# Splitting x into high and low parts at other places, and a later first y for 256 columns, in an attention and two-layer MoE kernel

## The chip, the cores and the metric

One Trainium2 chip, one core of it. The metric is the device time of one execution in microseconds (us); lower is better.

## What is computed

Attention with a window, and behind it two dense layers of the form y = g(x @ w_in) @ w_out, all in float32:

```python
# q, k, v: (4, 8, 576, 64)
scores = scale * np.matmul(q, k.transpose(0, 1, 3, 2))
mask = (rel >= 0) & (rel < 128)
scores = np.where(mask, scores + bias[None], -1000000000.0)
attn = np.exp(scores - np.max(scores, axis=-1, keepdims=True))
attn = attn / (np.sum(attn, axis=-1, keepdims=True) + 1e-09)
x = np.matmul(attn, v)            # -> x: (2304, 512)
h = x @ w_in;  x = (h * np.cos(h)) @ w_out          # first layer, 512 -> 2048 -> 512
h = x @ w_in2
g = np.where(h >= 1, h, np.where(h <= -1, 0.0, (h + 1) ** 2 / 4.0))
out = g @ w_out2
```

## The kernel before

**Attention.** The work is cut into 36 pairs: two blocks of 128 tokens and two heads. `pairs[n]` has b0 = 2 (n // 4) and hp = n % 4. The loop of `attention()` runs in steps k from -3 to 31, each of which holds four pairs in different stages, and its last pair (35) and what is left of pairs 31 to 34 are written out by hand behind the loop (the tail, p0 to p4 = pairs 31 to 35). In step k:

- PE: `pe_s` (L248) the scores of pair k + 3, `pe_t` (L288) eight transposes of the attention weights of pair k, `pe_v` (L313) the outputs of pair k - 1;
- DVE: `scores` (L263) adds the bias and takes the maximum of pair k + 3 in two halves; ACT makes the exponentials (L270) with their sums in st;
- `prepare` (L446, POOL) adds 1e-9 to the sums, `invert` (L451, DVE) takes the reciprocal, `normalise` (L276, POOL) multiplies, two instructions a pair;
- `copy_t` (L297 ACT, L299 DVE) brings the transposes out of PSUM as pt, by the string PT;
- `put_x` (L333 ACT, L335 DVE) brings the output of pair k - 1 out of PSUM into x;
- `make(0)` in the steps of D_STEPS does one piece of the first layer's weights (below).

For k < 1 the three of `prepare`, `invert` and `normalise` stand between the two halves of `scores` (L481 to L485).

**x in two parts.** A float32 matmul is done as three matmuls of a high part (float32r, rounded) and the low part (what is left): hi x hi, hi x lo, lo x hi. The first layer's first pass (`chunks[0]`) takes 768 columns: part 0 of 512 (tokens of pairs 0 to 7) and part 1 of 256 (pairs 8 to 11), each in four tiles d. For part 1, `put_x` writes the high part on ACT straight out of PSUM (L326) and `sub_lo` (L81, DVE) the low part behind it, in the same step (k = 9 to 12). For part 0, `split_x` (ACT cast L353, DVE L81) does both parts of one d. The low parts of part 0 lie where the bias tables lie that pairs with hp = d still need, so d = 0 and 1 are split in steps 30 and 31, and d = 2 and 3 in the tail.

**The first pass.** `moes()` runs f = 0 to 15 over blocks of 128 of the 2048. For each f: `mm_a` of part 0 (L375, h, 12 matmuls of 512 columns), `chain` of part 0 (ACT L387 k, DVE L389, ACT L391 sine, DVE L393 t, ACT L405 gh, DVE L81 gl), `mm_b` of part 0 for f - 1 (L425, y, 12 matmuls), then the same of part 1 with 256 columns (one tile g for both parts; `mm_b` 12 matmuls). PSUM has eight banks, y0 to y3 and h0 to h3. Part 1's y lies in h2 and h3, but for f = 1 part 0's h lies in h3 too:

```python
            tag = "h3" if f == 1 and i == 0 else f"h{i}"
```

Between these stand `slot()` and `make(0)`: pieces of the weights, which come as 64-bit numbers and are made float32 and split (DVE L125, L131, L135, L81; ACT L114, L140), eight pieces for each f. Their loads (L91) are issued on SP and need a buffer that L135 frees. All other chunks follow behind the first pass and run the same way with 512 columns.

**What sets the order.** `manual_schedule` keeps the instructions of PE, DVE, ACT, POOL and SP as they are written; each engine runs its own in that order, and waits where a tile isn't ready or its buffer not free.

Of the kernel before, what the change touches and what calls it, by code (L numbers as in the profile page):

```python
# [43 lines left out]
def attention_moe_moe_kernel(  # L44
# [35 lines left out]
    def sub_lo(eng, out, full, hi):  # L80
        eng.tensor_tensor(out=out, in0=full, in1=f32(hi), op=ALU.subtract)  # L81
# [114 lines left out]
    def new_x(w, dtype=F32):  # L196
        size = w if x_free[w] else 512
        slot = size, x_free[size].pop(0)
        return one.tile([128, size], dtype, tag=f"x{size}.{slot[1]}", name=nm("x"))[:, 0:w], slot
# [115 lines left out]
                              start=(i == 0), stop=(i == nb - 1))  # L315

    evicted = [0]

    def put_x(p, eng=None):
        t0 = p["b0"] * 128  # L320
        o, w = max(a for a in all_parts if a[0] <= t0)
        if (o, w) == chunks[0]["parts"][1]:
            hi, slot = new_x(w, F32R)
            lo = x_lo(4 + p["hp"])
            chunks[0]["xs", 1, p["hp"]] = hi, lo, slot
            ACT.copy(hi, p["vb"][:, 0:256])  # L326
            sub_lo(DVE, lo, p["vb"][:, 0:256], hi)
            return
        if (o, p["hp"]) not in x_tiles:
            x_tiles[o, p["hp"]] = new_x(w)  # L330
        x = x_tiles[o, p["hp"]][0][:, t0 - o:t0 - o + 256]
        if (eng or XE[evicted[0] % len(XE)]) == "A":
            ACT.copy(x, p["vb"][:, 0:256])  # L333
        else:
            DVE.tensor_copy(x, p["vb"][:, 0:256])  # L335
        evicted[0] += 1
# [8 lines left out]
            free_x(c["xs", i, d][2])  # L345

    def split_x(c, i, ds):
        o, w = c["parts"][i]
        for d in ds:
            x, slot = x_tiles.pop((o, d))  # L350
            hi, hi_slot = new_x(w, F32R)
            lo = x_lo(4 * i + d)[:, 0:w]
            ACT.copy(hi, x)  # L353
            sub_lo(DVE, lo, x, hi)
            free_x(slot)
            c["xs", i, d] = hi, lo, hi_slot

    h_no = [-1]

# [93 lines left out]
    def attention():  # L453
        qk, v = slice(0, 640), slice(640, 1024)
        for part in (qk, v):
            for n in range(3):
                load(n, part)
        make_identity(nc, ident)
        make_dist8()
        DVE.memset(half, 0.5)  # L460
        DVE.memset(half_pi, TWO_PI / 4)
        np_ = len(pairs)
        c0 = chunks[0]
        for k in range(-AHEAD, np_ - AHEAD - 1):
            new = pairs[k + AHEAD]
            mid = pairs[k + AHEAD - 1] if k + AHEAD >= 1 else None
            nrm = pairs[k + AHEAD - 2] if k >= 2 else None
            cur = pairs[k] if k >= 0 else None
            old = pairs[k - 1] if k >= 1 else None
            if k > -AHEAD:  # L470
                load(k + AHEAD + 1)
                load(k + AHEAD + 2)
            if k == 0:
                pe_t(cur)
            pe_s(new)
            if k > 0:
                pe_t(cur)
            if old:
                pe_v(old)
            scores(new, 0)  # L480
            if k < 1 and mid:  # L481

                prepare(mid)
                invert(mid)
                normalise(mid)  # L485
            if cur:
                copy_t(cur, 0)
            if nrm:
                normalise(nrm)
            if k >= 1:  # L490
                prepare(mid)
            scores(new, 1)

            if k in D_STEPS:
                make(0)
            if k in (np_ - 6, np_ - 5):
                split_x(c0, 0, [k - (np_ - 6)])
            if k >= 1:
                invert(mid)
            if cur:  # L500
                copy_t(cur, 1)
            if k + 1 == D_STEPS[0]:
                start(0)
            if old:
                put_x(old)

        p0, p1, p2, p3, p4 = pairs[np_ - 5:]
        pe_s(p4)
        pe_t(p1)
        pe_v(p0)  # L510
        scores(p4, 0)
        copy_t(p1, 0, "D")
        normalise(p2)
        invert(p3, add=True)
        normalise(p3)
        copy_t(p1, 1, "A")
        scores(p4, 1)
        pe_t(p2)
        pe_v(p1)
        copy_t(p2, 0, "D")  # L520

        ACT.activation(half_pi2, half, AF.Sin)
        put_x(p0, "A")
        invert(p4, add=True)
        normalise(p4)
        copy_t(p2, 1, "D")
        pe_t(p3)
        pe_v(p2)
        split_x(c0, 0, [2])
        put_x(p1, "D")  # L530
        copy_t(p3, 0, "D")
        copy_t(p3, 1, "A")
        pe_t(p4)
        pe_v(p3)
        put_x(p2, "A")
        split_x(c0, 0, [3])
        copy_t(p4, 0, "D")
        copy_t(p4, 1, "A")
        make(0)
        make(0)  # L540
        pe_v(p4)
        put_x(p3, "A")
        for _ in range(D_TAIL - 2):
            make(0)
        put_x(p4, "A")

    def moes():
# [7 lines left out]
        for f in range(NF):  # L555
# [16 lines left out]
                free_xs(c0, 1)  # L572
            while made[0] < min(N_W1, 8 * f + 9):
                make(0)
            if f:
                mm_b(c0, 1, f - 1)
        carried = c0
        step = 0
        for ci, c in enumerate(chunks[1:], 1):
# [81 lines left out]
```

## Time and profile before

| | |
|---|---|
| median of 3 runs | 930.52 us (930.34 to 932.04) |
| profiled execution | 930.21 us, its span 928.4 us |
| busy, share of the span | PE 98%, DVE 59%, ACT 47%, POOL 13% |
| attention, up to the first matmul of the first pass | 127.84 us |
| DMA queue of the loads, share of 16 engines | 22.9% |
| granted TensorE clock | 0.999 |

Times in the rows below are microseconds from the span's start. A row of a timeline gives start, duration, engine, line, operation, the tile written <- the tiles read, the shape, how many instructions were merged, and in brackets how long the engine stood before it and what ended that.

### The profile page before, as it was taken

How to read it: one execution, taken by the hardware profiler on the slowest of the kernel's cores; microseconds unless marked ns; L12 is line 12 of the kernel's file. 1: busy time of each engine (PE TensorE's matmuls, PEld its weight loads, DVE VectorE, ACT ScalarE, POOL GpSimd, SP SyncE). 2: the span in 40 equal slices, each digit the busy share in tenths (PEclk: the TensorE clock that was granted, in tenths of full speed). 3: DMA queues.
4: the chain of work that ended last, by engine and by line, in shares of the span. 5: the costliest groups of instructions: out<-in, count | busy, mean ns of one | idle time of the engine just before them, and what ended most of it. 6: DMA issues, size and time to landing. Idle time of an engine off the chain costs nothing.

```text
span 928.4 us, 13106 instructions
## 1 busy us (share of the span) xinstructions
PE 909.6 (98%) x4944; PEld 755.2 (81%) x4944; DVE 551.6 (59%) x1192; ACT 435.2 (47%) x923; POOL 120.8 (13%) x147
## 2 busy tenths in 40 slices
PE   7999988999999999999999999999999999999998
PEld 5767777888888888888888888888888888888898
DVE  6888788888868667767433543344344334433443
ACT  7788865665655444444455532232233223322332
POOL 5666620000000000000144510000000000000000
PEclk9999999999999999999999999999999999999999
DMA  9346013333305443542322200010001000100100
GB/s 355 145 168 265 2 67 116 116 128 120 116 34 191 136 151 122 170 137 92 102 100 104 69 1 1 0 46 1 1 1 45 1 1 1 46 0 1 39 9 23
DMA packets 24687, 74.77 MB, mean 81 GB/s; under 512 B 2736, under 2 KB 3632, under 8 KB 24624
## 3 DMA queue, kind: packets, MB, share of 16 engines
q1 hardware_dynamic: 24624, 73.94, 22.9%
q8 instruction: 39, 0.64, 0.3%
q14 instruction: 24, 0.20, 0.1%
HBM read 60.82 MB, written 13.11 MB: 80 GB/s over the span
## 4 chain that ended last, share of the span: by engine, by line
PE 79%; DVE 10%; ACT 8%; issue 2%; POOL 0%; DMA 0%; ACTq 0%; DVEq 0%
PE y L425 36%; PE h L375 36%; PE pa L248 2%; PE pa L288 2%; PE pa L313 2%; DVE wu L131 2%; ACT t L391 2%; ACT sc L270 2%; DVE t L393 1%; ACT wh L140 1%; DVE wl L81 1%; DVE gl L81 1%; DVE wu L135 1%; ACT wu L114 1%; ACT gh L405 1%
## 5 line engine op out<-in xcount | busy, mean ns | idle before, releaser
L375 PE MATMUL h<-x,wh 128*128 128x512 f32 (+1 forms) x640 | 237.0, 370 | 1.0
L375 PE MATMUL h<-xl,wh 128*128 128x512 f32 (+1 forms) x640 | 235.6, 368 | 0.0
L375 PE MATMUL h<-x,wl 128*128 128x512 f32 (+1 forms) x640 | 235.5, 368 | 0.0
L425 PE MATMUL y<-gl,wh 128*128 128x512 f32 (+1 forms) x576 | 217.5, 378 | 0.4 <-DVE gl L81 0.4
L425 PE MATMUL y<-gh,wh 128*128 128x512 f32 (+1 forms) x576 | 217.3, 377 | 0.0
L425 PE MATMUL y<-gh,wl 128*128 128x512 f32 (+1 forms) x576 | 217.3, 377 | 0.0
L396 ACT ACTIVATE t<-t,half 128x512 f32<-128x512 f32 (+1 forms) x80 | 54.4, 680 | 189.7 <-DVE t L395 189.4
L375 PEld LDWEIGHTS h<-x,wh 128*128 128x128 f32 x640 | 120.6, 188 | 23.6 <-DVE t L393 3.2
L375 PEld LDWEIGHTS h<-x,wl 128*128 128x128 f32 x640 | 120.7, 189 | 20.3
L375 PEld LDWEIGHTS h<-xl,wh 128*128 128x128 f32 x640 | 120.6, 188 | 20.1
L81 DVE TENSOR_TENSOR gl<-t,gh 128x512 fp32r<-128x512 f32 (+1 forms) x144 | 95.5, 663 | 68.3 <-ACT gh L405 64.1
L405 ACT CAST gh<-t 128x512 fp32r<-128x512 f32 (+1 forms) x144 | 86.0, 597 | 105.0 <-DVE t L398 56.4
L425 PEld LDWEIGHTS y<-gl,wh 128*128 128x128 f32 x576 | 108.5, 188 | 21.0 <-DVE gl L81 1.1
L425 PEld LDWEIGHTS y<-gh,wh 128*128 128x128 f32 x576 | 108.4, 188 | 20.0
L425 PEld LDWEIGHTS y<-gh,wl 128*128 128x128 f32 x576 | 108.3, 188 | 19.9
L395 DVE TENSOR_SCALAR t<-h 128x512 f32<-128x512 f32 (+1 forms) x80 | 50.9, 636 | 88.9 <-PE h L375 88.8
L81 POOL TENSOR_TENSOR wl<-wst,wh 128x512 fp32r<-128x512 f32 x32 | 41.1, 1308 | 372.6 <-ACT wh L182 372.6
L398 DVE TENSOR_TENSOR t<-h,t 128x512 f32<-128x512 f32 (+1 forms) x80 | 51.1, 638 | 61.8 <-ACT t L396 61.8
L391 ACT ACTIVATE t<-t,half_pi 128x512 f32<-128x512 f32 x80 | 54.6, 682 | 62.6 <-DVE t L389 62.6
L389 DVE SCALAR_TENSOR_TENSOR t<-h,k 128x512 f32<-128x512 f32 x80 | 50.8, 635 | 54.6 <-ACT k L387 54.4
L270 ACT ACTIVATE sc<-sc,st 128x256 f32<-128x256 f32 (+1 forms) x144 | 70.2, 489 | 23.9 <-DVE st L263 20.5
L276 POOL TENSOR_TENSOR sc<-sc,st 128x512 f32<-128x512 f32 (+1 forms) x72 | 70.0, 994 | 35.3 <-DVE st L451 30.5
(56 smaller groups left out, 853.1 us busy)
## 6 DMA issues: line engine op xcount, KB each, us to landing
wst<-in_w SPq DMA_DIRECT2D x64, 512.0 KB, 3.7
qkv<-in_qkv SPq DMA_DIRECT2D x33, 512.0 KB, 9.4
wd<-wu SPq DMA_DIRECT2D x32, 256.0 KB, 2.4
wst<-wd SPq DMA_DIRECT2D x16, 512.0 KB, 3.3
out_t<-ys SPq DMA_DIRECT2D x16, 256.0 KB, 2.1
qkv<-in_qkv SPq DMA_DIRECT2D x3, 320.0 KB, 3.6
qkv<-in_qkv SPq DMA_DIRECT2D x3, 192.0 KB, 5.1
out_t<-ys SPq DMA_DIRECT2D x4, 128.0 KB, 1.8
```

What stands on the lines that cost most here:

```text
L81: eng.tensor_tensor(out=out, in0=full, in1=f32(hi), op=ALU.subtract)
L131: DVE.scalar_tensor_tensor(out=ui, in0=high, scalar=0x80000000, in1=ui, op0=ALU.bitwise_and, op1=ALU.bitwise_or)
L270: ACT.activation(sc[:, h, 0:w], sc[:, h, 0:w], AF.Exp, bias=st[:, c:c + 1], scale=-1.0, accum_out=st[:, 4 + c:5 + c])
L276: POOL.tensor_tensor(out=sc[:, :, 0:w], in0=sc[:, :, 0:w], in1=st[:, 8 + 2 * j:10 + 2 * j].unsqueeze(2).to_broadcast([128, 2, w]), op=ALU. ...
L375: PE.matmul(h, lhsT=a[:, 0, s], rhs=x, start=(n == 0), stop=(n == 11))
L389: DVE.scalar_tensor_tensor(out=t, in0=h, scalar=INV_2PI, in1=k, op0=ALU.mult, op1=ALU.subtract)
L391: ACT.activation(t, t, AF.Sin, bias=half_pi, scale=TWO_PI)
L395: DVE.tensor_scalar(out=t, in0=h, scalar1=-1.0, scalar2=1.0, op0=ALU.max, op1=ALU.min)
L396: ACT.activation(t, t, AF.Square, bias=half, scale=0.5)
L398: DVE.tensor_tensor(out=t, in0=h, in1=t, op=ALU.max)
L405: ACT.copy(gh, t)
L425: PE.matmul(c["y", i][d], lhsT=a[:, 1, s], rhs=x, start=(f == 0 and k == 0 and not (i and d % 2)), stop=(f == NF - 1 and k == 2 and (i == ...
```

## The change

Five edits, all in the order of instructions:

- for k < 1, the sum of 1e-9 is done on DVE (`invert(mid, add=True)`) and stands with the reciprocal and POOL's product behind both halves of `scores`;
- the low parts of part 1 are put on a list and done in the next step, behind the second half of `scores` and the piece of weights;
- `split_x` is cut into `split_hi` (ACT's cast) and what it returns (`rest`, DVE's low part). The casts of d = 0, 1, 2 stand at the ends of steps 29, 30, 31; the low parts of 0 and 1 in steps 30 and 31;
- in the tail the low parts of 2 and 3 stand behind the last copies, and one piece of weights stands before these copies. There are still five pieces in the tail;
- in the first pass `mm_b` of part 1 for f - 1 = 0 isn't done in f = 1 but in f = 2, before that for f - 1 = 1.

```diff
--- before.py
+++ after.py
@@ -315,6 +315,7 @@
                               start=(i == 0), stop=(i == nb - 1))
 
     evicted = [0]
+    low_parts = []
 
     def put_x(p, eng=None):
         t0 = p["b0"] * 128
@@ -324,7 +325,7 @@
             lo = x_lo(4 + p["hp"])
             chunks[0]["xs", 1, p["hp"]] = hi, lo, slot
             ACT.copy(hi, p["vb"][:, 0:256])
-            sub_lo(DVE, lo, p["vb"][:, 0:256], hi)
+            low_parts.append(lambda: sub_lo(DVE, lo, p["vb"][:, 0:256], hi))
             return
         if (o, p["hp"]) not in x_tiles:
             x_tiles[o, p["hp"]] = new_x(w)
@@ -345,15 +346,23 @@
             free_x(c["xs", i, d][2])
 
     def split_x(c, i, ds):
+        for d in ds:
+            split_hi(c, i, d)()
+
+    def split_hi(c, i, d):
+
         o, w = c["parts"][i]
-        for d in ds:
-            x, slot = x_tiles.pop((o, d))
-            hi, hi_slot = new_x(w, F32R)
+        x, slot = x_tiles.pop((o, d))
+        hi, hi_slot = new_x(w, F32R)
+        ACT.copy(hi, x)
+
+        def rest():
             lo = x_lo(4 * i + d)[:, 0:w]
-            ACT.copy(hi, x)
             sub_lo(DVE, lo, x, hi)
             free_x(slot)
             c["xs", i, d] = hi, lo, hi_slot
+
+        return rest
 
     h_no = [-1]
 
@@ -478,11 +487,6 @@
             if old:
                 pe_v(old)
             scores(new, 0)
-            if k < 1 and mid:
-
-                prepare(mid)
-                invert(mid)
-                normalise(mid)
             if cur:
                 copy_t(cur, 0)
             if nrm:
@@ -493,17 +497,23 @@
 
             if k in D_STEPS:
                 make(0)
-            if k in (np_ - 6, np_ - 5):
-                split_x(c0, 0, [k - (np_ - 6)])
-            if k >= 1:
-                invert(mid)
+            while low_parts:
+                low_parts.pop()()
+            if mid:
+                invert(mid, add=k < 1)
+                if k < 1:
+
+                    normalise(mid)
             if cur:
                 copy_t(cur, 1)
             if k + 1 == D_STEPS[0]:
                 start(0)
             if old:
                 put_x(old)
-
+            if k >= np_ - 7:
+                low_parts.append(split_hi(c0, 0, k - (np_ - 7)))
+
+        x2, = low_parts
         p0, p1, p2, p3, p4 = pairs[np_ - 5:]
         pe_s(p4)
         pe_t(p1)
@@ -526,20 +536,21 @@
         copy_t(p2, 1, "D")
         pe_t(p3)
         pe_v(p2)
-        split_x(c0, 0, [2])
         put_x(p1, "D")
         copy_t(p3, 0, "D")
         copy_t(p3, 1, "A")
         pe_t(p4)
         pe_v(p3)
         put_x(p2, "A")
-        split_x(c0, 0, [3])
+        make(0)
         copy_t(p4, 0, "D")
         copy_t(p4, 1, "A")
+        x2()
+        pe_v(p4)
+        x3 = split_hi(c0, 0, 3)
+        put_x(p3, "A")
         make(0)
-        make(0)
-        pe_v(p4)
-        put_x(p3, "A")
+        x3()
         for _ in range(D_TAIL - 2):
             make(0)
         put_x(p4, "A")
@@ -572,8 +583,8 @@
                 free_xs(c0, 1)
             while made[0] < min(N_W1, 8 * f + 9):
                 make(0)
-            if f:
-                mm_b(c0, 1, f - 1)
+            for g in (f - 2, f - 1) if f == 2 else (f - 1,) if f > 2 else ():
+                mm_b(c0, 1, g)
         carried = c0
         step = 0
         for ci, c in enumerate(chunks[1:], 1):
```

Line numbers of the changed kernel are up to ten higher (L81 is the same; L451 is L460, L450 L459, L335 L336, L375 L384, L425 L434).

DVE in step 11, from the last scores of pair 14 on (sc and st are tiles of `scores`, xl are low parts of x, wu and wst weights). Before:

```order
L135 SCALAR_TENSOR_TENSOR wu_355<-wst_353,wu_355 128x512
L451 RECIPROCAL st_679<-st_679 128x4
L299 COPY pt_781<-pa_745 128x512
L81 TENSOR_TENSOR xl_784<-pa_750,x_783 128x256
L263 ISA sc_817,st_789<-pa_790,xl_108 128x256
```

And now:

```order
L135 SCALAR_TENSOR_TENSOR wu_355<-wst_353,wu_355 128x512
L81 TENSOR_TENSOR xl_726<-pa_697,x_725 128x256
L460 RECIPROCAL st_678<-st_678 128x4
L299 COPY pt_781<-pa_744 128x512
L263 ISA sc_816,st_788<-pa_789,xl_108 128x256
```

The low part of pair 10 (xl_784) is gone from this step's end, and that of pair 9 (xl_726), whose high part ACT made in the step before, stands in front of the reciprocal.

DVE in the tail, from the second copy of pair 33 on (pt are copies, x_1692 is x of a later chunk, xl_1898 and xl_1927 or xl_1929 and xl_1949 the low parts of d = 2 and 3). Before:

```order
L299 COPY pt_1876<-pa_1853 128x512
L81 TENSOR_TENSOR xl_1898<-x_357,x_1897 128x512
L335 COPY x_1692<-pa_1858 128x256
L299 COPY pt_1902<-pa_1878 128x512
L81 TENSOR_TENSOR xl_1927<-x_410,x_1926 128x512
L299 COPY pt_1930<-pa_1906 128x512
L131 SCALAR_TENSOR_TENSOR wu_1037<-wst_404,wu_1037 128x512
```

And now:

```order
L299 COPY pt_1878<-pa_1855 128x512
L336 COPY x_1692<-pa_1860 128x256
L299 COPY pt_1900<-pa_1880 128x512
L131 SCALAR_TENSOR_TENSOR wu_1037<-wst_404,wu_1037 128x512
L299 COPY pt_1925<-pa_1904 128x512
L81 TENSOR_TENSOR xl_1929<-x_357,x_1800 128x512
L135 SCALAR_TENSOR_TENSOR wu_1037<-wst_404,wu_1037 128x512
L81 TENSOR_TENSOR xl_1949<-x_410,x_1940 128x512
```

No low part stands between the copies that PE's transposes and outputs wait for; one piece of weights (L131) stands there.

PE in the first pass, f = 2, from the last matmul of part 1's h on (y_2183 and y_2184 hold part 1's y, g_2017 is g of f = 0 and g_2098 that of f = 1). Now:

```order
L384 MATMUL h_2149<-x_835,wl_2014 128x256
L434 MATMUL y_2183<-g_2017,wh_776 128x256 x2
L434 MATMUL y_2183<-g_2017,wl_777 128x256
L434 MATMUL y_2183<-g_2017,wh_776 128x256 x2
L434 MATMUL y_2183<-g_2017,wl_777 128x256
L434 MATMUL y_2184<-g_2017,wh_776 128x256 x2
```

Before, the twelve matmuls of g_2017 stood in f = 1, right in front of h of f = 2; now h of f = 2 and y of part 0 run first.

## Rows read from the trace of the kernel before

**Rows 1.** The page's first part, PE: busy us, share of the span, instructions.

```profile
PE 909.6 (98%) x4944; PEld 755.2 (81%) x4944; DVE 551.6 (59%) x1192; ACT 435.2 (47%) x923; POOL 120.8 (13%) x147
```

**Rows 2.** Waits in 0 to 125 us: total, times, longest.

```profile
DVE xl L81 <- ACT x L326: 4.7, 4, 1.5
DVE xl L81 <- ACT x L353: 3.5, 3, 1.4
PE pa L288 <- DVE pt L299: 3.3, 3, 1.5
DVE st L451 <- POOL st L446: 2.7, 4, 1.0
```

**Rows 3.** Timeline of PE: first scores of steps 10, 15, 28 and 29.

```profile
41.00 1.13 PE L248 MATMUL pa<-qkv 64*128 64x256 f32 x8
...
59.79 0.92 PE L248 MATMUL pa<-qkv 64*128 64x256 f32 x8
...
100.55 1.13 PE L248 MATMUL pa<-qkv 64*128 64x256 f32 x8
...
103.67 1.13 PE L248 MATMUL pa<-qkv 64*128 64x256 f32 x8
```

**Rows 4.** Timeline of DVE: steps 9, 14 and 29.

```profile
42.29 0.42 DVE L81 TENSOR_TENSOR xl<-pa,x 128x256 fp32r<-128x256 f32 x1 [0.89 <-ACT x L326]
...
59.24 0.81 DVE L81 TENSOR_TENSOR wl<-wu,wh 128x512 fp32r<-128x512 f32 x1
...
104.40 0.42 DVE L263 CUSTOM_DVE_ANT_0 sc<-pa,xl 128x256 f32<-128x256 f32 x1 [0.52 <-PE pa L248]
```

**Rows 5.** Timeline of all engines, steps 0 and 1.

```profile
11.89 0.18 DVE L451 RECIPROCAL st<-st 128x4 f32<-128x4 f32 x1 [0.88 <-POOL st L446]
...
13.76 0.56 ACT L297 COPY pt<-pa 128x512 f32<-128x512 f32 x1
...
14.46 0.63 PE L288 MATMUL pa<-ident,sc 128*128 128x128 f32 x4 [0.28 <-ACT pt L297]
```

**Rows 6.** Timeline of all engines, steps 30 and 31 and the tail.

```profile
111.35 0.69 DVE L81 TENSOR_TENSOR xl<-x,x 128x512 fp32r<-128x512 f32 x1 [1.39 <-ACT x L353]
...
118.29 0.16 DVE L450 TENSOR_SCALAR st<-st 128x4 f32<-128x4 f32 x1
...
118.83 2.04 POOL L276 TENSOR_TENSOR sc<-sc,st 128x512 f32<-128x512 f32 x2 [0.46 <-DVE st L451]
...
120.19 1.28 ACT L522 ACT_TABLE_LOAD   x1
120.20 0.70 DVE L450 TENSOR_SCALAR st<-st 128x4 f32<-128x4 f32 x1 [0.28 <-ACT sc L270]
...
122.50 1.37 DVE L81 TENSOR_TENSOR xl<-x,x 128x512 fp32r<-128x512 f32 x1 [0.81 <-ACT x L353]
...
127.84 0.50 PE L375 MATMUL h<-x,wh 128*128 128x512 f32 x1
```

**Rows 7.** Timeline of PE in the first pass, f = 1 and 2.

```profile
142.75 0.50 PE L425 MATMUL y<-g,wh 128*128 128x256 f32 x2 [2.38 <-DVE t L393]
...
143.56 0.39 PE L375 MATMUL h<-x,wh 128*128 128x512 f32 x1
...
146.31 0.39 PE L425 MATMUL y<-gh,wh 128*128 128x512 f32 x1
```

**Rows 8.** Timeline of DVE in the first pass, f = 1, 2 and 13.

```profile
143.49 0.69 DVE L81 TENSOR_TENSOR gl<-t,gh 128x512 fp32r<-128x512 f32 x1 [0.20 <-issue]
...
150.82 0.69 DVE L393 TENSOR_TENSOR t<-h,t 128x512 f32<-128x512 f32 x1 [0.46 <-ACT t L391]
...
246.62 0.69 DVE L393 TENSOR_TENSOR t<-h,t 128x512 f32<-128x512 f32 x1 [0.46 <-ACT t L391]
```

**Rows 9.** Waits in 125 to 300 us: total, times, longest.

```profile
PEld h L375 <- DVE t L393: 3.2, 11, 0.3
```

**Rows 10.** Waits of SP's queue in 0 to 300 us: total, times, longest.

```profile
SPq L91 <- DVE wu L135: 206.8, 32, 51.3
```

## The prediction

> **What bounds the kernel now.** I read the page's first part first: PE is busy 909.6 of 928.4 us [rows 1]. That says PE, but the ends of matmuls are modelled, so a busy PE can hide waiting. So I went to the waits of two stretches, and from the longest of them to the timelines.
>
> In attention (to 127.84 us) DVE stands 4.7 us until ACT has cast the high parts of the 256 columns, 3.5 us for those of the 512 columns, and 2.7 us until POOL has added 1e-9; PE stands 3.3 us for DVE's copies pt [rows 2]. A step without such a wait takes PE 3.12 us (100.55 to 103.67). Steps 10 to 14, from 41.00 to 59.79, take 18.79 us instead of 5 x 3.12 = 15.60 [rows 3]. These are the steps in which DVE stands in front of the low part, with the next scores queued behind it [rows 4].
>
> In the first pass PE has one long stall, 2.38 us, in the first y of the 256 columns [rows 7], and 11 short ones, 3.2 us in all, each at the first matmul of a new f, until DVE's t (L393) has left h's bank [rows 9]. That L393 starts at 150.82 in f = 2 and at 246.62 in f = 13: 95.80/11 = 8.71 us a step [rows 8]. PE's own work is 24 matmuls of 0.229 us (12 run from 143.56 to 146.31 [rows 7]) and 24 of half of that: 8.25 us. So from f = 0 on the pace is that of DVE and ACT, which hand t, g and the weights to each other, and PE waits for them. Whatever time the pass ends is set by when that loop starts.
>
> **The change part by part.**
>
> Start (k < 1). The sum of 1e-9 moves from POOL to DVE and, with the reciprocal, behind the second scores. DVE's 0.88 us in front of the reciprocal at 11.89 go, and the reciprocal leaves that place [rows 5]. Then PE's first transposes, which need POOL's product, come some 0.1 later, as the reciprocal now stands behind two more scores. Pair 3's second scores come 0.9 earlier, so do ACT's exponentials and the copy at 13.76 [rows 5], and with it PE's transposes at 14.46, which had stood 0.28 for it. Ends: 0.3 (PE's own stall) and 2.7 (all of DVE's wait [rows 2]). I take **0.9**, nearest to the one wait that stands in front of PE; the others are covered by ACT's queue.
>
> The 256 columns (steps 9 to 13). Four low parts of 0.42 move one step on, behind the second scores. DVE's four waits, 4.7 us, go; the 0.42 are paid as before. Followed with the rows' durations: in step 10 the scores start at 41.7, not behind the low part of 42.29 (DVE starts scores 0.73 behind PE's matmuls, 104.40 against 103.67 [rows 3, 4]); step 10's scores end at 44.1, so PE's next scores find their banks free; step 12 starts at 47.2, step 13 at 50.5, step 14 at 53.7, step 15 at 56.6 instead of 59.79. In step 13 PE still stands some 0.2 for ACT's copy. The low part now holds the bank of v's output a step longer; that bank is written again two steps later, and each low part is done more than 1 us before that. ACT's hi is not moved here. Ends: 3.2 (18.79 to 15.60), and 0.8 if the slow steps belong to their three pieces of weight work, at most 0.81 each [rows 4]: 3.2 - 2.4. I take **3.1**, by the followed steps.
>
> The 512 columns (step 29 to the end of attention). The casts of d = 0, 1, 2 go to ACT one step sooner, the low parts of 0 and 1 stand behind the second scores, those of 2 and 3 behind the last copies. In step 30 DVE is through with its scores at 111.35 - 1.39 = 109.96 [rows 6]: low part to 110.6, reciprocal to 110.7, 1.3 sooner. ACT's copy no longer stands behind the cast, so PE's next transposes come 0.4 sooner. In step 31 DVE's low part ends at 113.6 and its last copy at 114.3; PE has pair 32's second transposes at 114.7. Then DVE's copies follow each other with no low part between them. Two holds stay: the 1e-9 for the last pair waits for POOL's products to about 118.4, and pair 34's second copy for the bank behind it. ACT's table load of 1.28 stays, from 117.8, where ACT isn't awaited. PE ends the outputs of pairs 34 and 35 at 122.9 and 123.95 and starts the pass there, not at 127.84. Low part 2 ends at 122.8 and 3 at 124.0, before the pass's 8th and 11th matmul want them. The five pieces of weights are the same five, so 14 pieces are made when the pass starts, as before.
> Check from above: from 103.67 [rows 3] to 127.84 [rows 6] PE has three steps of 3.12 and a tail of one scores, four transposes and five outputs of pairs, ten thirds of 3.12: 19.8 of 24.2 us, so 4.4 is the high end. Low end: PE's 3.3 us for pt [rows 2] less the table load 1.28: 2.0. I take **3.9** as followed, near the high end because PE then hardly waits.
> All that is moved starts the loop of the first pass as much earlier: its first L389 waits for the first h.
>
> The first pass. mm_b of the 256 columns for f = 0 (12 matmuls, 1.4 us) goes behind f = 2's; no instruction is added. The 2.38 go. In the times of before PE then starts h for f = 2 at 139.5 and is through at 142.2; next is y of the 512 columns of f = 1, whose gl DVE makes at 143.49 to 144.18 [rows 8]: a new wait of 1.2 for gh and 0.5 for gl. With the moved 1.4 us paid in f = 2, PE comes to h of f = 3 at about 151.0; L393 of f = 2 ends at 151.45, and at 151.9 PE starts it now. From there L393 of f = 3 decides, and no instruction of DVE or ACT in that loop waits for PE's y. Ends: 0, and 2.38 if the loop could follow. I take **0**: the stall is cut up and handed on.
>
> The sum: 0.9 + 3.1 + 3.9 + 0 = 7.9 us. The profiled execution took 930.21; that gives 922.3. It lies 0.31 below the median of the three runs, 930.52, so I give **922.6**. SP is passed by nothing: its loads for the weights wait for DVE to free their buffers (206.8 us [rows 10]), so they come earlier with it.
>
> **A rule against the change.** The sum moved to DVE, and every low part of 512 columns, runs beside POOL's products: the same 1e-9 on DVE took 0.16 at 118.29 and 0.70 at 120.20, ending as POOL's pair from 118.83 (2.04) ended; the same low part took 0.69 at 111.35 and 1.37 at 122.50 [rows 6]. The Trainium skill, "SBUF — State Buffer", section "Who interferes with whom", says why: VectorE's second port belongs to GpSimd too, and the second to come is blocked for the whole instruction. The trace agrees. In my sum stand two such holds, of 0.5 each (start and tail), neither of which ends last. By the rule alone each would be paid in full, 6.9 in place of 7.9.
>
> **The rivals.**
> 1. *The stall of 2.38 comes off as well*, because DVE and ACT could follow a PE that doesn't stop in f = 1. For it: PE is 98% busy [rows 1], and this is its longest stall behind the first load. Against it: 8.71 us a step over eleven steps, with DVE and ACT alone in the loop [rows 8]. 930.5 - 7.9 - 2.4 = 920.2. It is what the Trainium skill's "Perfetto Trace Analysis", section "Optimization Strategy", would have one expect, which looks for the gaps of the most contended engine.
> 2. *Attention gives back half.* The weight work, not the low part, paces steps 11 to 14, ACT's table load gets into the tail's way, and the start yields only PE's own stall: the low ends 0.3 + 0.8 + 2.0 = 3.1, so 927.4. For it: three of the five slow steps do carry weight work. Against: the four DVE waits lie in exactly the slow steps.
> 3. *Slower, by POOL's hold.* One mechanism: DVE comes to a moved instruction while POOL's pair of products runs, and stands up to 2.04 us, with scores and copies queued behind. Seven can be hit (three sums, four low parts from SBUF): 14.3 us at most. It turns the sign if more than 7.9/14.3 = 55% of that is paid on the path; if 90%, 12.9: 935.5. Against: POOL starts right behind the reciprocal and ends 2.1 later, while the low part stands two scores and a copy behind, 2.3 in the followed step 31.
> 4. *No change.* The pass could run by the arrival of its weights and not by its start, 930.5. Against: SP's loads wait for DVE, not the other way [rows 10].
>
> **How the numbers follow.** Forecast 0.72, rival 1 0.08, rival 2 0.10, rival 3 0.04, rival 4 0.06. The range of the forecast is what its parts leave open, about 3 us either way: 919.5 holds rival 1, 926.0 a part of rival 2. Less than 0.2% (1.9 us) a measurement of this kernel can't tell from nothing: faster 0.72 + 0.08 + 0.10 = 0.90, same 0.06, slower 0.04.
>
> **What the new profile would show.** Right: DVE no longer waits for ACT's casts of x in attention; steps 10 to 14 take under 16 us; the first matmul of the pass stands near 120 us; the stall of 2.38 is gone, a wait for gh and gl of 1 to 2 us stands in f = 2, and L393 still comes every 8.7 us. Wrong: a first matmul later than 123.5, a step of the pass other than 8.7, or long sums and low parts on DVE beside POOL.

## The result

| | before | after |
|---|---|---|
| median | 931.25 us (930.34 to 932.04, 4 runs) | 923.47 us (923.07 to 924.23, 4 runs) |
| profiled execution | 930.21 us, span 928.4 | 923.45 us, span 921.7 |
| attention, to the first matmul of the first pass | 127.84 us | 121.05 us |

The changed kernel is faster: ratio 0.9918, 95% interval 0.9901 to 0.9935. Forecast were 922.6 us and a range of 919.5 to 926.0. An execution of the kernel before takes near 930.4 or near 932.0 us, so it is luck that the medians lie 7.78 apart, close to the 7.9 forecast; the profiled executions lie 6.76 apart. Attention holds 6.79.

The page's first part, after (beside [rows 1]):

```profile
PE 907.9 (99%) x4944; PEld 754.5 (82%) x4944; DVE 553.3 (60%) x1195; ACT 434.4 (47%) x923; POOL 120.4 (13%) x144
```

PE's busy time falls by 1.7 us and the span by 6.7, so the number that says "98% busy" hardly moved. Timeline of PE, after: first scores of steps 2 ("the third step" of the expectations, counted from k = 0), 10, 15 and 29, and the first matmul of the first pass (columns as in [rows 3]):

```profile
16.02 1.13 PE L248 MATMUL pa<-qkv 64*128 64x256 f32 x8
...
41.20 1.14 PE L248 MATMUL pa<-qkv 64*128 64x256 f32 x8
...
56.90 0.92 PE L248 MATMUL pa<-qkv 64*128 64x256 f32 x8
...
100.78 1.13 PE L248 MATMUL pa<-qkv 64*128 64x256 f32 x8
...
121.05 0.50 PE L384 MATMUL h<-x,wh 128*128 128x512 f32 x1
```

Steps 10 to 14 take 15.70 us, where they took 18.79 [rows 3]: 3.09 gained. From step 29 to the first pass it is 20.27, where it was 24.17 [rows 3, 6]: 3.90 gained. At step 10 the kernel is 0.20 later than before (41.20 for 41.00): that is the start, and it was lost, not won. Waits of DVE in 0 to 125 us, after:

```profile
DVE sc L263 <- PE pa L248: 5.1, 11, 1.7
DVE pt L299 <- PE pa L288: 3.6, 13, 0.6
```

The 4.7 and 3.5 us for ACT's casts and the 2.7 for POOL's sum [rows 2] are gone from the list; DVE waits for PE, somewhat longer than before (3.0 and 3.0 us). The first pass, after: timeline of PE in f = 2, then of DVE (t, once L393, is now L402) in f = 2 and 13.

```profile
136.67 0.50 PE L434 MATMUL y<-gh,wh 128*128 128x512 f32 x1 [1.06 <-ACT gh L414]
...
137.45 0.50 PE L434 MATMUL y<-gl,wh 128*128 128x512 f32 x1 [0.28 <-DVE gl L81]
```

```profile
144.04 0.69 DVE L402 TENSOR_TENSOR t<-h,t 128x512 f32<-128x512 f32 x1 [0.46 <-ACT t L400]
...
239.85 0.69 DVE L402 TENSOR_TENSOR t<-h,t 128x512 f32<-128x512 f32 x1 [0.46 <-ACT t L400]
```

PE's stall of 2.38 [rows 7] has become 1.06 + 0.28; the step is (239.85 - 144.04)/11 = 8.71 us, as before [rows 8]. The pass starts 6.79 earlier (121.05 for 127.84) and its f = 13 is reached 6.77 earlier.

### The profile page after: what moved, and what is told of

Its sections match the earlier page's. It is cut to its first block, busy times and chain, and to the rows that moved or that the text cites. A ratio compares the mean times of both kernels' runs of the same rounds, so it can differ in the third digit from the quotient of the medians.

```text
span 921.7 us, 13110 instructions
## 1 busy us (share of the span) xinstructions
PE 907.9 (99%) x4944; PEld 754.5 (82%) x4944; DVE 553.3 (60%) x1195; ACT 434.4 (47%) x923; POOL 120.4 (13%) x144
## 4 chain that ended last, share of the span: by engine, by line
PE 81%; DVE 8%; ACT 6%; issue 2%; DMA 1%; SPq 0%; POOL 0%; ACTq 0%; DVEq 0%; POOLq 0%
PE y L434 36%; PE h L384 36%; PE pa L248 3%; PE pa L288 3%; PE pa L313 3%; DVE wu L131 2%; ACT t L400 2%; DMA qkv<-in_qkv 1%; DVE t L402 1%; DVE wl L81 1%; DVE gl L81 1%; DVE wu L135 1%; ACT wh L140 1%; ACT gh L414 1%; ACT wu L114 1%
## 5 line engine op out<-in xcount | busy, mean ns | idle before, releaser
L384 PE MATMUL h<-x,wh 128*128 128x512 f32 (+1 forms) x640 | 237.1, 370 | 1.3 <-DVE t L402 0.2
L384 PE MATMUL h<-xl,wh 128*128 128x512 f32 (+1 forms) x640 | 235.6, 368 | 0.0
L384 PE MATMUL h<-x,wl 128*128 128x512 f32 (+1 forms) x640 | 235.5, 368 | 0.0
L434 PE MATMUL y<-gh,wh 128*128 128x512 f32 (+1 forms) x576 | 217.4, 378 | 1.1 <-ACT gh L414 1.1
L434 PE MATMUL y<-gl,wh 128*128 128x512 f32 (+1 forms) x576 | 217.6, 378 | 0.6 <-DVE gl L81 0.6
L434 PE MATMUL y<-gh,wl 128*128 128x512 f32 (+1 forms) x576 | 217.3, 377 | 0.0
L384 PEld LDWEIGHTS h<-x,wh 128*128 128x128 f32 x640 | 120.6, 189 | 24.3 <-DVE t L402 3.9
L384 PEld LDWEIGHTS h<-x,wl 128*128 128x128 f32 x640 | 120.6, 188 | 20.3
L384 PEld LDWEIGHTS h<-xl,wh 128*128 128x128 f32 x640 | 120.6, 188 | 20.0
L81 DVE TENSOR_TENSOR gl<-t,gh 128x512 fp32r<-128x512 f32 (+1 forms) x144 | 95.5, 663 | 68.3 <-ACT gh L414 64.1
L434 PEld LDWEIGHTS y<-gl,wh 128*128 128x128 f32 x576 | 108.4, 188 | 21.6 <-DVE gl L81 1.7
L434 PEld LDWEIGHTS y<-gh,wh 128*128 128x128 f32 x576 | 108.3, 188 | 21.5 <-ACT gh L414 1.5
L434 PEld LDWEIGHTS y<-gh,wl 128*128 128x128 f32 x576 | 108.4, 188 | 19.8
L81 POOL TENSOR_TENSOR wl<-wst,wh 128x512 fp32r<-128x512 f32 x32 | 41.1, 1309 | 371.1 <-ACT wh L182 371.1
L398 DVE SCALAR_TENSOR_TENSOR t<-h,k 128x512 f32<-128x512 f32 x80 | 50.8, 635 | 53.9 <-ACT k L396 53.7
```

Source lines behind the costliest of these rows:

```text
L384: PE.matmul(h, lhsT=a[:, 0, s], rhs=x, start=(n == 0), stop=(n == 11))
L398: DVE.scalar_tensor_tensor(out=t, in0=h, scalar=INV_2PI, in1=k, op0=ALU.mult, op1=ALU.subtract)
L434: PE.matmul(c["y", i][d], lhsT=a[:, 1, s], rhs=x, start=(f == 0 and k == 0 and not (i and d % 2)), stop=(f == NF - 1 and k == 2 and (i == ...
```

## The experiments

Theory: three waits of DVE were in front of PE in attention, each part of the change takes its own, and the first pass is paced by DVE and ACT, so that it only starts earlier. Open: why the start lost 0.2 where 0.9 were forecast. Eleven kernels ran. Times of one group were taken on one chip beside the kernel before (medians there 930.94, 930.33 and 930.42).

### One part undone at a time

**start_undone**

```diff
+            if k < 1 and mid:
+                prepare(mid)
+                invert(mid)
+                normalise(mid)
             if cur:
                 copy_t(cur, 0)
...
-            if mid:
-                invert(mid, add=k < 1)
-                if k < 1:
-                    normalise(mid)
+            if k >= 1:
+                invert(mid)
```

> The changed kernel with its start put back: for the first three pairs the sum of 1e-9 on POOL, the reciprocal and the products stand between the two halves of the scores again. Read from the changed kernel's chain: POOL's product of pair 0 starts 0.35 later (8.08 for 7.73), since the reciprocal now stands behind pair 1's second scores and DVE's own sum, PE's transposes of pair 0 and with them pair 3's scores come later, and the third step starts at 16.02 in place of 15.83. This theory: 0.2 us faster than the changed kernel (923.3 for 923.5), third step at 15.83 again, first matmul of the first pass at 120.85. The prediction's term (the new start is worth 0.9): slower, 924.4, third step near 16.9. Rival 2's low end (0.3): 923.8.

**cols256_undone**

```diff
-            low_parts.append(lambda: sub_lo(DVE, lo, p["vb"][:, 0:256], hi))
+            sub_lo(DVE, lo, p["vb"][:, 0:256], hi)
```

> The changed kernel with the four low parts of the 256 columns back behind their casts, in the step of the cast. The prediction (that wait alone is the 3.1 us of steps 10 to 14): those five steps take 18.8 us again in place of 15.7, first matmul of the first pass at 124.1 in place of 121.05, time 926.6. Rival 2 (weight work paces these steps): at most 0.8 slower, 924.3. If the parts of the change share one wait, less than 3.1 here and the rest elsewhere.

**cols512_undone**

```diff
             while low_parts:
                 low_parts.pop()()
+            if k in (np_ - 6, np_ - 5):
+                split_x(c0, 0, [k - (np_ - 6)])
...
-            if k >= np_ - 7:
-                low_parts.append(split_hi(c0, 0, k - (np_ - 7)))
...
+        split_x(c0, 0, [2])
         put_x(p1, "D")
...
+        split_x(c0, 0, [3])
         copy_t(p4, 0, "D")
         copy_t(p4, 1, "A")
-        x2()
+        make(0)
+        make(0)
         pe_v(p4)
-        x3 = split_hi(c0, 0, 3)
         put_x(p3, "A")
-        make(0)
-        x3()
```

> The changed kernel with the casts and low parts of the 512 columns where they stood before (casts of d = 0 and 1 a step later with the low part behind them, d = 2 and 3 between the last copies). The prediction: 3.9 us slower, 927.4, steps up to 29 unchanged, first matmul of the first pass at 124.95. Rival 2 (the table load and the last copies pace the tail): 2.0 slower, 925.5.

**defer_undone**

```diff
-            for g in (f - 2, f - 1) if f == 2 else (f - 1,) if f > 2 else ():
-                mm_b(c0, 1, g)
+            if f:
+                mm_b(c0, 1, f - 1)
```

> The changed kernel with y of the 256 columns for f = 0 back in f = 1. The prediction (the loop of DVE and ACT paces the pass): no difference, 923.5 within 0.3; PE's stall of some 2.4 us in f = 1 is back, the waits for gh and gl in f = 2 (1.06 and 0.28) are gone, t (L402) still every 8.71 us and at 239.85 in f = 13. Rival 1 (the stall comes off the time): 2.4 slower, 925.9.

Measured, with the start of step 2 and of the first pass's first matmul in each profile:

| kernel | median us | ratio to before | 95% | step 2 | first matmul | between |
|---|---|---|---|---|---|---|
| before | 931.25 | | | 15.83 | 127.84 | 112.01 |
| after | 923.47 | 0.9918 | 0.9901 to 0.9935 | 16.02 | 121.05 | 105.03 |
| start_undone | 923.75 | 0.9925 | 0.9913 to 0.9938 | 16.02 | 121.06 | 105.04 |
| cols256_undone | 925.90 | 0.9950 | 0.9937 to 0.9962 | 15.04 | 123.18 | 108.14 |
| cols512_undone | 927.12 | 0.9960 | 0.9947 to 0.9972 | 16.90 | 125.83 | 108.93 |
| defer_undone | 922.88 | 0.9910 | 0.9895 to 0.9925 | 16.28 | 121.32 | 105.04 |

The last column settles the two large terms. Without the new place of the 256 columns' low parts it is 3.11 us longer, without that of the 512 columns 3.90; 3.11 + 3.90 = 7.01, and before it was 6.98 longer: the terms add, neither shares a wait with the other. Rival 2's low ends (0.8 and 2.0) fall. The times alone would not show this so well: the profiled executions of the two (925.68 and 928.20) are 2.23 and 4.75 slower than that of the changed kernel, since their starts are 0.98 sooner and 0.88 later. Timelines of PE, of cols256_undone (steps 10 and 15) and then of cols512_undone (step 31, the tail's scores 3.58 behind it where a free step takes 3.12, and the first matmul):

```profile
40.24 1.13 PE L248 MATMUL pa<-qkv 64*128 64x256 f32 x8
...
59.03 0.92 PE L248 MATMUL pa<-qkv 64*128 64x256 f32 x8
```

```profile
107.93 1.13 PE L248 MATMUL pa<-qkv 64*128 64x256 f32 x8
...
111.51 1.31 PE L248 MATMUL pa<-qkv 64*128 64x256 f32 x8
...
125.83 0.50 PE L384 MATMUL h<-x,wh 128*128 128x512 f32 x1
```

Steps 10 to 14 take 18.79 us again, to the hundredth. With the first y of the 256 columns back in f = 1, PE's stall is back too, and costs nothing. Timeline of PE, defer_undone, f = 1:

```profile
136.25 0.80 PE L434 MATMUL y<-g,wh 128*128 128x256 f32 x2 [2.35 <-DVE t L402]
```

From t of f = 0 to t of f = 13 it takes 113.49 us (126.72 to 240.21), in the changed kernel 113.41 (126.44 to 239.85). The median is 0.6 us under that of the changed kernel, on other chips and with overlapping intervals; 2.4 slower, as rival 1 had it, is excluded. But the column "step 2" holds a surprise: after, cols256_undone, cols512_undone and defer_undone have the same start, instruction for instruction, and reach step 2 at 16.02, 15.04, 16.90 and 16.28. start_undone alone settles nothing about the start: it was expected to reach step 2 at 15.83 and came at 16.02, behind first scores that began 0.17 later than the changed kernel's (4.06 for 3.89). So from here on the start is measured from its first scores.

### What the start is worth, and PE's clock

Mean ns of one 64x256 matmul (L248) and of the transposes tells PE's clock: 631 ns in the first microseconds of every profile without added work, 402 to 428 later. The granted clock reads 1.00 in that first stretch (last section); that PE is at the lower level there is inferred from the durations: from 11 to 13 us, where the granted clock reads 0.50 in warm_old_start and slot_moved (both below), the same matmul takes 623 and 661 ns. Timelines of PE between the first scores and step 2, of after, of cols256_undone and of start_undone (there from pair 0's last transposes on):

```profile
3.89 4.21 PE L248 MATMUL pa<-qkv 64*128 64x128 f32 x24 [3.89 <-DMA qkv<-in_qkv]
8.75 0.69 PE L288 MATMUL pa<-ident,sc 128*128 128x128 f32 x2 [0.65 <-POOL sc L276]
9.75 1.12 PE L288 MATMUL pa<-ident,sc 128*128 128x128 f32 x4 [0.31 <-POOL sc L276]
10.80 3.21 PE L248 MATMUL pa<-qkv 64*128 64x128 f32 x16
```

```profile
3.79 4.00 PE L248 MATMUL pa<-qkv 64*128 64x128 f32 x24 [3.79 <-DMA qkv<-in_qkv]
8.64 0.44 PE L288 MATMUL pa<-ident,sc 128*128 128x128 f32 x2 [0.86 <-POOL sc L276]
9.64 0.65 PE L288 MATMUL pa<-ident,sc 128*128 128x128 f32 x4 [0.56 <-POOL sc L276]
10.23 2.80 PE L248 MATMUL pa<-qkv 64*128 64x128 f32 x16
```

```profile
9.58 0.67 PE L288 MATMUL pa<-ident,sc 128*128 128x128 f32 x4 [0.38 <-POOL sc L276]
10.18 1.79 PE L248 MATMUL pa<-qkv 64*128 64x128 f32 x12
12.97 1.04 PE L248 MATMUL pa<-qkv 64*128 64x256 f32 x4 [1.00 <-DVE st L263]
```

Pair 0's four transposes take 1.12 us in the changed kernel and 0.65 in cols256_undone, with the same instructions ahead of them: there the clock had risen. Pair 3's scores stand behind these transposes on PE, and DVE stands for them. Timeline of DVE, after (in cols256_undone the same wait is 0.93):

```profile
11.63 0.29 DVE L263 CUSTOM_DVE_ANT_0 sc<-pa,xl 128x128 f32<-128x128 f32 x1 [1.70 <-PE pa L248]
```

In the old order PE then stands 1.00 us for DVE anyway, so a slow PE costs it nothing there. Whether PE's clock decides was tried by giving PE work before the first load.

**warm_new_start**

```diff
+        warm = small("warm", shape=(128, 128))
+        DVE.memset(warm, 0.0)
+        wb = ps.tile([128, 512], F32, tag="h3", name=nm("warmb"))[:, 0:128]
+        for _ in range(7):
+            PE.matmul(wb, lhsT=warm, rhs=warm, start=True, stop=True)
         make_identity(nc, ident)
```

> The changed kernel with seven products of 128x128 zeros on PE, into a bank that nobody reads, while PE waits for its first load. Why: from the first scores to the third step the profiles took 12.13, 12.12, 12.83 and 11.25 us with one and the same new start, and 11.95 and 11.96 with the old one; in the run with 11.25 the 64x256 matmuls fell from 631 to 416 ns and the transposes from 0.69 to 0.44 (two) already near 7.5 us, in the changed kernel near 13, in the run with 12.83 after 15. Theory: the order of the start is worth what was predicted, but PE's clock rises late or early, and a PE that is let wait for POOL's products keeps the low level longer; with PE at work before the first load the rise comes before the first transposes, the third step stands at most 11.3 after the first scores, some 0.9 less than in the changed kernel: 922.6. Rival (the order alone makes the start what it is): 12.1 again and 923.5.

**warm_old_start**: the same lines in start_undone.

> The same seven products ahead of the old start (sum on POOL, reciprocal and products between the two halves of the scores, for the first three pairs), all else as in the changed kernel. At an equal, early clock the two orders can be compared: the prediction's term says that this one is 0.9 slower than warm_new_start (third step 12.1 after the first scores, 923.5); its low end 0.3; if the order is worth nothing, the same 922.6.

**scores_first**

```diff
-            if k == 0:
-                pe_t(cur)
             pe_s(new)
-            if k > 0:
+            if cur:
                 pe_t(cur)
```

> The changed kernel with pair 3's scores ahead of pair 0's transposes on PE, as in every later step. In the changed kernel's chain PE's transposes wait for POOL's products (to 9.75), pair 3's scores stand behind them at 10.80, and DVE is idle for 1.70 until it has them; nothing in those scores needs the products, only the banks of pair 2's scores, free at 9.0. Theory (the chain from POOL's product through PE to DVE sets the start): DVE's 1.70 go in the main, the third step comes 0.5 to 1.2 sooner, 922.6. Rival (PE's clock alone sets it): PE at work earlier brings the rise earlier, or the third step is where it was, 923.5.

Measured: warm_new_start 922.63 us (ratio 0.9912, 0.9898 to 0.9925), warm_old_start 923.59 (0.9926, 0.9913 to 0.9938), scores_first 922.46 (0.9911, 0.9897 to 0.9924). From the first scores to step 2, over all profiles (the four that begin with "slot" are described further below):

| start | profile | us to step 2 | PE's clock |
|---|---|---|---|
| old | before, start_undone | 11.95, 11.96 | high from about 9 us |
| old | warm_old_start | 11.94 | high at 6, low from 9.8 to 13 |
| new | warm_new_start | 11.02 | high from about 5.5 |
| new | cols256_undone | 11.25 | high from about 7.5 |
| new | slot_moved_defer_undone | 11.26 | high from 8.8 at the latest |
| new | slot_moved | 11.73 | high from about 7, low from 10.4 to 13.9 |
| new | after, defer_undone | 12.13, 12.12 | high from about 13 |
| new | cols512_undone | 12.83 | high only after 15 |
| new, scores first | scores_first | 11.32 | high from about 12.5 |
| new, scores first | slot_scores_first | 11.33 | high from about 6.5, low from 10 to 13.5 |
| new, scores first | slot_scores_first_warm | 10.93 | high from about 4, low from 11 to 13.5 |

The old order takes 11.95 in all three profiles, though the clock fell in one of them; the new one goes from 11.02 to 12.83 with the time of the rise. Over the six profiles of the new start without added work the mean is 11.89, so on average it was worth next to nothing (0.06). Timeline of PE, warm_new_start, then warm_old_start:

```profile
1.03 3.36 PE L471 MATMUL warmb<-warm 128*128 128x128 f32 x14 [1.03 <-DVE warm L468]
...
8.95 0.44 PE L288 MATMUL pa<-ident,sc 128*128 128x128 f32 x2 [1.48 <-POOL sc L276]
...
15.34 1.13 PE L248 MATMUL pa<-qkv 64*128 64x256 f32 x8
```

```profile
9.84 1.11 PE L288 MATMUL pa<-ident,sc 128*128 128x128 f32 x4 [0.56 <-POOL sc L276]
...
16.26 1.14 PE L248 MATMUL pa<-qkv 64*128 64x256 f32 x8
```

So the term of 0.9 exists where the clock is high. With the added work, which lets the first scores start some 0.4 later in both, it is 11.94 - 11.02 = 0.92 (by the medians 0.96, with intervals that overlap a little); without it 11.95 - 11.25 = 0.70 in cols256_undone. warm_old_start isn't quite the comparison at equal clocks that it was meant to be, since its clock fell back behind PE's wait; that its 11.94 agrees with the two others says that this costs the old order nothing. A slow clock turns the gain into a loss of 0.2 to 0.9, and which it is differs between executions of one start. The Trainium skill, "TensorE: Matmul & The Clock Gate", section "Part 1: The HAM clock gate", says that throttled is PE's default state, that activity lifts it, and that the number of slow matmuls varies between runs of a kernel; the rows above agree.

scores_first takes the other way: with pair 3's scores ahead, DVE's wait of 1.70 goes (one of 0.99 for the transposes comes), though all this runs at the low clock. Timeline of PE, scores_first:

```profile
9.09 1.65 PE L248 MATMUL pa<-qkv 64*128 64x128 f32 x8 [0.94 <-DVE st L263]
10.67 1.54 PE L288 MATMUL pa<-ident,sc 128*128 128x128 f32 x6
...
15.26 1.13 PE L248 MATMUL pa<-qkv 64*128 64x256 f32 x8
```

Step 2 comes 0.8 sooner behind the first scores than in the changed kernel (11.32 for 12.13), inside the 0.5 to 1.2 expected. That is no sooner than the plain order comes at the high clock (11.02 to 11.26).

### What paces the first pass

**slot_moved**

```diff
-            for _ in chain(c0, 0, f):
+            for n, _ in enumerate(chain(c0, 0, f)):
                 slot()
+                if n == 1:
+                    slot()
...
             for _ in chain(c0, 1, f):
                 slot()
             slot()
-            slot()
```

> The changed kernel with one piece of weight work of each f of the first pass moved on DVE: one of the two behind the 256 columns' chain goes between L398 and L402 of the 512 columns, where DVE waits 0.46 for ACT's sine in every f. No instruction is added, PE's order stays. Theory (the loop of DVE and ACT paces the pass, not PE's 8.25 and not the arrival of weights): the period falls from 8.71 by up to 0.46, to no less than 8.25, so 14 steps give up to 6.4 us: 917 to 923. Rival (the pass is paced by PE or by the arrival of its weights): 8.71 again, 923.5.

**slot_moved_defer_undone**: slot_moved with the diff of defer_undone.

> slot_moved with y of the 256 columns for f = 0 back in f = 1. In slot_moved the loop of DVE and ACT has come down to 7.9 to 8.0 us a step while it is ahead, and from f = 7 on t (L402) comes every 8.34 us with no wait of PE left between its matmuls: PE now sets the pace. Theory (a stall of PE costs only where PE sets the pace): the stall of some 2.4 us in f = 1 is now paid, less the waits of 0.24 and 0.28 in f = 2 that go: 1.5 to 2.4 slower than slot_moved, 918.6 to 919.5. Rival (the place of that y costs nothing in any case): 917.1.

Measured: slot_moved 917.12 us (0.9853, 0.9840 to 0.9867), slot_moved_defer_undone 918.10 (0.9865, 0.9848 to 0.9881). Timeline of DVE, slot_moved, t of f = 0, 6, 7 and 13:

```profile
126.01 0.69 DVE L402 TENSOR_TENSOR t<-h,t 128x512 f32<-128x512 f32 x1
...
173.65 0.68 DVE L402 TENSOR_TENSOR t<-h,t 128x512 f32<-128x512 f32 x1
...
181.85 0.69 DVE L402 TENSOR_TENSOR t<-h,t 128x512 f32<-128x512 f32 x1
...
231.89 0.69 DVE L402 TENSOR_TENSOR t<-h,t 128x512 f32<-128x512 f32 x1
```

No instruction was added, none taken away, PE's order stayed, and from the first matmul of the pass to the last of the program it is 790.92 us (120.63 to 911.55) for the changed kernel's 796.67 (121.05 to 917.72): 5.75 less. The rest of the 6.35 between the medians is the start and the chip. DVE no longer stands 0.46 in front of t. The six steps of t from 126.01 to 173.65 take 7.94 each, those from f = 7 on 50.04/6 = 8.34. PE goes at 8.34 from f = 3 on. Timeline of PE, slot_moved, first h of f = 3 and 9:

```profile
143.17 0.40 PE L384 MATMUL h<-x,wh 128*128 128x512 f32 x1
...
193.21 0.40 PE L384 MATMUL h<-x,wh 128*128 128x512 f32 x1
```

That is 50.04 us for six steps; in the changed kernel they took 52.26 (144.78 to 197.04), 8.71 each. There PE's weight loads waited 13 times for t, 3.9 us in all (120 to 250 us); here they wait for it no more, and ACT waits 20 times for h (18.3 us) where it waited once (1.6). So the loop of DVE and ACT is now the faster one: t catches up with PE until f = 6 and then goes at PE's pace. That loop fell by 0.77, more than the 0.46 expected and below the 8.25 given as the least: a second wait, 0.39 in front of the 256 columns' g, went as well, and one of 0.43 came in front of their t; the rest isn't accounted for. Windows of slot_moved (stretch, its length, busy time of PE, PEld, DVE, ACT and POOL, granted clock, DMA share, GB/s):

```profile
181.85:231.89 50.04, 50.04 (x290) 44.28 (x289) 45.31 (x85) 31.27 (x60) 0.00 (x0) 1.00 0.40 127
```

So 8.71 was the loop of DVE and ACT, as the prediction had it, and PE's own step is 8.34, a little above the 8.25 counted there.

Now that PE sets the pace, the place of the first y counts. Timeline of PE, slot_moved_defer_undone, f = 1:

```profile
134.28 0.50 PE L434 MATMUL y<-g,wh 128*128 128x256 f32 x2 [1.58 <-DVE t L402]
```

From t of f = 0 to t of f = 13 it takes 106.60 us (125.56 to 232.16) for slot_moved's 105.88: 0.72 slower, and 0.98 by the medians, with intervals that overlap. Expected were 1.5 to 2.4; the sign is right, the size was taken from the stall of 2.35, which a quicker DVE had already cut to 1.58, and slot_moved itself stands 0.52 in f = 2. So the same edit was worth nothing in the changed kernel and is worth some 0.7 to 1.0 behind this one: in its own kernel it is early, not useless.

### A version that beats both

**slot_scores_first**: the diffs of slot_moved and scores_first together.

> slot_moved with pair 3's scores ahead of pair 0's transposes on PE. The two edits lie in different stretches, so by the theory their gains add: scores_first took the third step to 11.32 us behind the first scores, slot_moved alone has it at 11.73 (its clock rose near 7.5 and fell back near 10), the changed kernel at 12.13: 0.4 to 0.8 less than slot_moved, 916.3 to 916.7. Rival (the start is PE's clock alone): 917.1.

**slot_scores_first_warm**: with the seven products of warm_new_start as well.

> slot_scores_first with the seven products of zeros on PE before the first load as well. Theory (clock and order both count): the third step comes less than 11.0 us behind the first scores, the least of all runs; but the products end 0.4 us after the load has come, so 0 to 0.7 less than slot_scores_first: 915.7 to 916.5. Rival (with the scores first PE does not wait long enough for the clock to matter): no less than slot_scores_first, and 0.4 more where the products hold the first scores back.

Measured: 916.51 us (0.9846, 0.9832 to 0.9861) and 916.68 (0.9848, 0.9834 to 0.9863). The first is the fastest of all kernels that ran: 13.9 us under the kernel before, and about 7 under the changed one. Its median is 0.6 under that of slot_moved, inside the 0.4 to 0.8 expected, but on another chip and with overlapping intervals; step 2 stands at 15.18, and slot_moved_defer_undone, with the plain order and a high clock, had it at 15.16. That the 0.6 comes from the order is therefore likely, not shown. The products bring nothing on top in time: step 2 comes 10.93 behind the first scores, the least of all, as the theory had it, but these start later, so it stands at 15.11 for 15.18, and the clock falls back behind the 1.91 us that PE waits ahead of pair 3's scores. Timeline of PE, slot_scores_first_warm:

```profile
10.05 0.97 PE L288 MATMUL pa<-ident,sc 128*128 128x128 f32 x6
...
12.97 1.41 PE L288 MATMUL pa<-ident,sc 128*128 128x128 f32 x6
```

Six transposes take 0.97 us and, 3 us later, 1.41; the granted clock is 0.50 from 11 to 14. For the time the rival was right.

## Why the prediction was right, and where not

- **What bounds the kernel.** Right: DVE's waits for ACT's casts stood in front of PE, and the pass runs at the pace of DVE and ACT (slot_moved). PE's own step was a little mis-sized, 8.25 for 8.34.
- **256 columns, 3.1 forecast.** 3.09 in the profile, 3.11 by cols256_undone. The step starts were followed as 47.2, 50.5, 53.7 and 56.6 for steps 12 to 15; they came at 47.43, 50.77, 54.00 and 56.90, with the start's 0.20 in them. The steps as written give 59.79 - 56.6 = 3.2, and 3.1 was taken; that it agrees within 0.02 is closer than the working.
- **512 columns, 3.9 forecast.** 3.90 in the profile, 3.90 by cols512_undone.
- **First pass, 0 forecast.** Right: every 8.71 us, a new wait of 1.06 + 0.28 for gh and gl (forecast 1.2 and 0.5), and no difference without the edit (defer_undone).
- **Start, 0.9 forecast, -0.19 measured: the step that failed.** The prediction counted DVE's wait in front of PE's second transposes as saved, and PE's first transposes as 0.1 later. They came 0.35 later (8.75 for 8.40), and it overlooked that pair 3's scores stand behind them on PE. Timeline of PE, before:

```profile
8.40 0.69 PE L288 MATMUL pa<-ident,sc 128*128 128x128 f32 x2
```

  Chain of waits of the changed kernel, pieces in order (start, us, what):

```profile
7.75 0.19 DVE st L460
...
8.08 1.62 POOL sc L276 x2
...
9.75 1.12 PE pa L288 x4
10.87 1.64 PE pa L248 x8
```

  The chain runs from pair 0's reciprocal through POOL and PE to DVE, and 2.76 us of it are PE at the low clock. With PE at the high clock the term is there (0.70 to 0.92); its size hung on a clock that none of the rows read for it priced. The sum 7.9 less 0.9 less 0.19 is 6.8, which is what was measured.
- **Rival 1** fell for the changed kernel. The Trainium skill's "Perfetto Trace Analysis", section "Optimization Strategy", sends one to the gaps of the most contended engine; here the longest gap behind the first load, on an engine 98% busy, was worth 0 us until another loop had been shortened, and then 0.7 to 1.0.
- **Rivals 2 and 4** fell: attention gave 6.79 and not 3.1, and the interval excludes no change.
- **Rival 3** fell in its price. DVE was held beside POOL's products in three places, off the chain. Timeline of DVE and POOL, after: the sum of pair 1 in the start; then, in the tail, the last sum, a piece of weights beside a product and the same piece alone.

```profile
8.93 0.79 DVE L459 TENSOR_SCALAR st<-st 128x4 f32<-128x4 f32 x1
...
114.91 0.69 DVE L459 TENSOR_SCALAR st<-st 128x4 f32<-128x4 f32 x1 [0.24 <-ACT sc L270]
...
115.99 2.04 POOL L276 TENSOR_TENSOR sc<-sc,st 128x512 f32<-128x512 f32 x2 [0.41 <-DVE st L460]
...
117.24 1.33 DVE L131 SCALAR_TENSOR_TENSOR wu<-wst,wu 128x512 uint32<-128x512 uint32 x1
...
122.90 0.68 DVE L131 SCALAR_TENSOR_TENSOR wu<-wst,wu 128x512 uint32<-128x512 uint32 x1
```

  Three holds of 0.5 to 0.65 each (a sum that isn't held takes 0.16 or 0.17), where the prediction's sum had two; the tail's sum was held before as well [rows 6]. All four low parts of 512 columns take 0.68 or 0.69 now. Long sums were among the prediction's signs of being wrong; they came and cost nothing that shows: the first delays pair 1's reciprocal, which isn't in the chain above, and the time from step 29 on came out as followed.

## What to carry to other kernels

Follow the engines' queues step by step with the durations of the rows: two terms found that way came out within 0.1 us, while the term that was read off a single wait had the wrong sign, since it left out what stood behind the later instruction on its engine. A stall is worth what its engine's pace is worth: ask first which loop sets the step, and find the wait inside that loop; moving one piece of DVE's work gave 5.75 us, nearly as much as the whole change. And a start that makes PE wait can pay for it in PE's clock, differently in each execution, so compare such edits by many runs or from a fixed event in the trace.

## What was not expected of the hardware

- The granted clock of a stretch doesn't show PE's first slow stretch: it reads 1.00 from 9.75 to 13.00 us in the changed kernel, where 64x256 matmuls take 637 ns, while a later fall does show. Windows of after, then of slot_moved, where the clock rose near 7 and fell behind PE's waits of 1.16 and 0.56:

```profile
9.75:13.00 3.25, 3.25 (x16) 2.39 (x17) 1.54 (x9) 1.82 (x9) 1.61 (x2) 1.00 1.02 411
```

```profile
10.40:13.90 3.50, 3.50 (x17) 2.48 (x16) 2.60 (x15) 2.46 (x11) 1.95 (x4) 0.51 1.02 413
```

- 0.51 is the lower of the two levels (1.2 of 2.4 GHz) for nearly all of 3.5 us, with PE busy throughout. PE had waited as long in warm_new_start (1.48 and 0.56) without a fall. What decides it was not tried.
- PE's own step in the first pass is 8.34 us where it waits for nothing, 1% above the 8.25 counted for its 48 matmuls. Those of 256 columns were counted at half of 0.229; they follow each other every 0.12 (twelve from 123.90 to 125.34 in the changed kernel), which gives 24 x 0.229 + 24 x 0.12 = 8.38.
